# Gram products of 320-column rows: the last piece as columns 192 to 319 instead of 256 to 319

## The chip, the cores and the metric

The kernel runs on one core of a Trainium2 chip. The metric is the device time of one execution in microseconds; three runs of the kernel before gave 719.22, 720.55 and 721.73 us, with the median 720.55 us. A profile of one execution was taken as well.

## The reference

Three layers follow one another, in float32.

```python
# a recurrence over 768 steps, for 4 batches x 8 heads of 40
m_new = np.maximum(f_gate + m, i_gate)
f_stab, i_stab = np.exp(f_gate + m - m_new), np.exp(i_gate - m_new)
C = f_stab * C + i_stab * outer(v_t, k_t)
n = f_stab * n + i_stab * k_t
y_t = sigmoid(o_gate) * (C @ q_t) / max(abs(n . q_t), 1)
# x: the 3072 rows of 320 (8 heads x 40)
h = x @ w_in                                   # 320 -> 2048
x = (max(h, 0) + alpha * min(h, 0)) @ w_out    # 2048 -> 320
out = max(x @ w1, x @ w2, x @ w3) @ w4         # 320 -> 768 -> 320
```

The inputs are float32; the host passes the weights as 64-bit words, so each weight is a float64 that the kernel turns into float32 itself.

## The kernel before

**Parts.** The rows are cut into 24 tiles of 128 tokens and eight chunks of three tiles. For each tile the recurrence is computed in its chunked form ("attention": products q by k, a matrix of decays db, a carried state C). The result is transposed into xT. Then come, chunk by chunk, the units m1 (x by w_in, eight matmuls of 384 columns into one PSUM bank, 16 units a chunk), m2 (g by w_out), and four chunks later m3 (three products and a maximum, 18 units a chunk) and m4 (h by the last weight, w4). All large products are made of float16 parts with a high and a low half, for precision.

**Scales and Gram products.** To split a weight into float16 halves the kernel needs a power of two that bounds it. `Norms` (line 1172) finds one with TensorE: for each converted block of a weight it multiplies the block's transpose by the block itself, 128 columns at a time, and adds all of these in one PSUM bank; the diagonal then holds sums of squares of columns. `power` (line 1193) takes the largest entry, spreads it over the partitions by a product with ones, and halves the exponent. Only the exponent's bound matters. For w_in and the weights w1 to w3 the blocks have 512, 256 or 128 columns, so all pieces are 128 wide. In `prep_rows` (line 1258) the blocks are rows of 320 columns: 16 blocks of w_out and 6 of w4. Their pieces are columns 0 to 127, 256 to 319 (64 wide) and 128 to 255, in this order. In the profile and in the order these products are those whose only input is a buffer cv, qs or ks: the buffers in which a weight is converted.

**Order.** Nothing is issued as it is written. Each operation is recorded with its inputs and outputs (`Sched.add`, line 154), and `Sched.cost` (line 225) gives it a duration by its shape: a matmul's grows with its output columns. `Sched.order` (line 305) lays out the program with these durations, from six sets of starting values and in eight rounds each, and keeps the plan with the shortest planned end. The plan sets the order on all five queues (TensorE, DVE, ACT, POOL and the transfers of SP), which of the eight PSUM banks each product uses, on which of two engines some copies run, and where TensorE gets fillers: products of ones with themselves (line 569), put in front of an instruction where the plan has TensorE idle and its clock low. 26 fillers open the program; others follow only after the plan's first stretch.

So the cost of one product can move any instruction.

Of the kernel before, what the change touches and what calls it, by code (L numbers as in the profile page):

```python
# [585 lines left out]
def kernel(  # L586
# [26 lines left out]
    class Ring:  # L613
# [6 lines left out]
        def __call__(self):  # L620
            self.n += 1
            t = self.t + self.more
            return t[(self.n - 1) % len(t)]
# [548 lines left out]
    class Norms:  # L1172
# [6 lines left out]

        def __call__(self, v):  # L1180

            at = list(range(0, v.shape[1], 128))
            for c in sorted(at, key=lambda c: (c > 0, min(128, v.shape[1] - c))):
                w = min(128, v.shape[1] - c)
                pe.matmul(
                    out=self.ps[0:w, self.at, 0:w], lhsT=v[:, c:c + w], rhs=v[:, c:c + w],
                    start=(self.k == 0), stop=(self.k == self.n - 1),
                )
                self.k += 1
            if self.k == self.n:  # L1190
                self.at, self.k = self.at + 1, 0
# [167 lines left out]
    for j in range(NCH + LAG):  # L1359
# [20 lines left out]
        if j == AFTER[3]:  # L1380
            prep_rows(w4, wp_s, wp, 2, 4, 8, sbp)
            dve.scalar_tensor_tensor(
                out=kw, in0=rw[:, 7:8], scalar=ONE, in1=rw[:, 8:9], op0=ALU.mult, op1=ALU.mult
# [79 lines left out]
```

## Time and profile before

| what | value |
|---|---|
| median of the runs | 720.55 us (719.22 to 721.73) |
| span of the profiled execution | 717.8 us |
| from the span to the median | 2.75 us |
| TensorE (PE) | 685.9 us busy, 96% |
| weight loads (PEld) | 464.1 us, 65% |
| DVE | 484.9 us, 68% |
| ACT | 415.8 us, 58% |
| POOL | 159.4 us, 22% |
| mean granted clock of TensorE | 0.950 |

The profiled execution's own time is known by its span, from the first instruction to the last; what lies around it is taken as the distance to the median. The busy shares are means over stages: in the first hundred microseconds the weights are converted and the first tiles go through attention; then attention and the first layer's units run side by side; in the last half TensorE has nothing but large products. A granted clock of 1.0 is 2.4 GHz, 0.5 is 1.2 GHz. The durations of matmuls overlap, so what one costs is read from the distance between starts.

### The profile page before, as it was taken

What the parts mean: (1) busy time and instruction counts of PE and PEld (TensorE: products, weight loads), DVE (VectorE), ACT (ScalarE), POOL (GpSimd) and SP (SyncE); (2) the same over time, 40 slices, a digit from 0 to 9 for tenths busy, and PEclk for the clock granted to TensorE, in tenths of its full rate; (3) what the DMA queues carried; (4) which work ended last, traced back from release to release, by engine and by line L of the source; (5) the groups of instructions that cost most, each with busy time, mean ns of one, the idle gap of its engine ahead of it and who ended that gap; (6) DMA issues with size and microseconds to landing.
All of it is one profiled execution on the core that took longest, in us unless ns stands there. A gap on an engine that the chain in (4) does not pass through costs nothing.

```text
span 717.8 us, 14674 instructions
## 1 busy us (share of the span) xinstructions
PE 685.9 (96%) x5299; PEld 464.1 (65%) x5299; DVE 484.9 (68%) x1256; ACT 415.8 (58%) x983; POOL 159.4 (22%) x193
## 2 busy tenths in 40 slices
PE   4789999999899999999999999999999999999998
PEld 3678766666566666666666666666766676666665
DVE  7676879999799899899579963786265223242332
ACT  4667769899799889887467662662253122222222
POOL 1221242044251362166014310330031000000000
PEclk8555799999999999999999999999999999999999
DMA  8865476565794656863443362122201110002000
GB/s 251 280 189 188 154 225 190 165 194 161 230 292 123 203 168 182 244 190 92 104 137 119 122 136 88 45 64 38 59 19 33 28 50 12 28 1 61 8 21 27
DMA packets 82802, 88.33 MB, mean 123 GB/s; under 512 B 38754, under 2 KB 66218, under 8 KB 82730
## 3 DMA queue, kind: packets, MB, share of 16 engines
q1 hardware_dynamic: 82730, 87.40, 42.2%
q8 instruction: 41, 0.67, 0.4%
q14 instruction: 31, 0.25, 0.1%
HBM read 60.83 MB, written 8.75 MB: 97 GB/s over the span
## 4 chain that ended last, share of the span: by engine, by line
PE 59%; DVE 2%; issue 0%; DMA 0%; SPq 0%; ACT 0%; ACTq 0%
PE bank L574 59%; DMA cs<-cpd 0%; SPq L574 0%; DVE wq L574 0%; DVE h L574 0%; DVE hl L574 0%; DVE vw L574 0%; DVE g L574 0%; DVE cp L574 0%; ACT db L574 0%; DVE y L574 0%; DVE gf L574 0%; DVE xs L574 0%; DVE cv L574 0%; ACT ob L574 0%
## 5 line engine op out<-in xcount | busy, mean ns | idle before, releaser
L574 PE MATMUL bank<-xT,wi 128*128 128x384 f16 x1024 | 177.1, 328 | 0.2 <-DVE gf L574 0.2
L574 PE MATMUL bank<-wo,g 128*128 128x320 f16 x1152 | 165.3, 299 | 0.6 <-DVE g L574 0.6
L574 PEld LDWEIGHTS <-wq 128*128 128x128 f16 x1152 | 110.9, 98 | 71.2 <-issue 0.5
L574 PEld LDWEIGHTS <-g 128*128 128x128 f16 x1152 | 110.9, 98 | 44.8 <-DVE g L574 0.9
L574 PEld LDWEIGHTS <-wi 128*128 128x128 f16 x1024 | 98.8, 98 | 62.3 <-issue 2.0
L574 PE MATMUL bank<-x2T,wq 128*128 128x384 f16 x720 | 123.1, 326 | 0.4 <-DVE gf L574 0.4
L574 POOL TENSOR_TENSOR g<-gf,g 128x384 f16<-128x384 f32 x63 | 60.6, 964 | 174.1 <-DVE g L574 95.3
L574 DVE TENSOR_TENSOR mv<-bank,mv 128x384 f32<-128x384 f32 x96 | 52.9, 551 | 60.4 <-PE bank L574 59.5
L574 DVE SCALAR_TENSOR_TENSOR gf<-d,al,bank 128x384 f32<-128x384 f32 x128 | 76.5, 603 | 9.9 <-ACT d L574 9.1
L574 ACT ACTIVATE h<-mv 128x384 f16<-128x384 f32 x47 | 24.5, 521 | 94.1 <-DVE mv L574 94.1
L574 ACT ACTIVATE d<-bank 128x384 f32<-128x384 f32 x128 | 61.1, 479 | 20.1 <-PE bank L574 18.8
L574 PE MATMUL bank<-xT,wq 128*128 128x384 f16 x432 | 70.7, 326 | 0.0
L574 ACT ACTIVATE db<-db,gtok 128x128 f32<-128x128 f32 x192 | 63.4, 390 | 9.1 <-POOL db L574 8.9
L574 ACT ACTIVATE g<-gf 128x384 f16<-128x384 f32 x104 | 53.7, 519 | 20.0 <-DVE gf L574 19.7
L574 PE MATMUL bank<-wp,h 128*128 128x320 f16 x432 | 61.0, 299 | 0.0
L574 PEld LDWEIGHTS <-h 128*128 128x128 f16 x432 | 42.1, 98 | 16.7
L574 POOL TENSOR_TENSOR h<-mv,h 128x384 f16<-128x384 f32 x14 | 13.8, 983 | 161.1 <-ACT h L574 161.0
L574 DVE TENSOR_TENSOR g<-gf,g 128x384 f16<-128x384 f32 x65 | 39.2, 610 | 11.3 <-ACT g L574 11.1
L574 POOL TENSOR_SCALAR_AFFINE_SELECT db<-db 128x512 f32<-128x512 f32 x48 | 36.7, 784 | 40.5 <-ACT gm L574 25.8
L574 DVE TENSOR_TENSOR db<-bank,db 128x512 f32<-128x512 f32 x48 | 31.8, 682 | 7.3 <-PE bank L574 2.0
L574 DVE TENSOR_SCALAR sx<-sx 128x1 int32<-128x1 int32 x48 | 7.0, 146 | 40.5 <-ACT xs L574 40.2
L574 ACT ACTIVATE xs<-bank 128x320 f16<-128x320 f32 x24 | 10.3, 429 | 37.1 <-PE bank L574 36.5
(170 smaller groups left out, 890.3 us busy)
## 6 DMA issues: line engine op xcount, KB each, us to landing
db<-ddr SPq DMA_DIRECT2D x24, 512.0 KB
raw<-tok SPq DMA_DIRECT2D x18, 480.0 KB
kv<-tok SPq DMA_DIRECT2D x24, 320.0 KB
q<-qk SPq DMA_DIRECT2D x36, 160.0 KB
raw<-w_out SPq DMA_DIRECT2D x16, 320.0 KB
raw<-w SPq DMA_DIRECT2D x9, 512.0 KB
qs<-hl SPq DMA_DIRECT2D x54, 80.0 KB
ks<-hl SPq DMA_DIRECT2D x54, 80.0 KB
```

The source lines that it names most:

```text
L574: getattr(e, meth)(**{k: v.on(v.bank.tile) if isinstance(v, View) else v for k, v in kw.items()})
```

## The change

The pieces of a row are now taken in the order of their columns, and each is 128 wide: the last one of 320 columns starts at 192 instead of 256. Columns 192 to 255 are thus counted twice, and their sums of squares come out larger; the bound is still one. Blocks whose width is a multiple of 128 are cut as before.

```diff
         def __call__(self, v):
 
-            at = list(range(0, v.shape[1], 128))
-            for c in sorted(at, key=lambda c: (c > 0, min(128, v.shape[1] - c))):
-                w = min(128, v.shape[1] - c)
+            for c in range(0, v.shape[1], 128):
+                c = min(c, v.shape[1] - 128)
                 pe.matmul(
-                    out=self.ps[0:w, self.at, 0:w], lhsT=v[:, c:c + w], rhs=v[:, c:c + w],
+                    out=self.ps[:, self.at, :], lhsT=v[:, c:c + 128], rhs=v[:, c:c + 128],
                     start=(self.k == 0), stop=(self.k == self.n - 1),
                 )
                 self.k += 1
```

Since the recorded durations of 22 products differ, the plan differs from its first instructions on. Three places on TensorE's queue follow.

The first place is just ahead of the first m1 unit. Before, a row of w_out in cv is taken in three pieces, and then come 15 fillers, of which the first stands here, and the unit:

```order
L574 LDWEIGHTS cv_137
L574 MATMUL bank_66<-cv_137 128x128
L574 LDWEIGHTS cv_137
L574 MATMUL bank_66<-cv_137 64x64
L574 LDWEIGHTS cv_137
L574 MATMUL bank_66<-cv_137 128x128
L569 LDWEIGHTS ones
L569 MATMUL bank_67<-ones 128x256
```

Now attention products (C by q) and pieces of a row in ks stand there, and the unit follows at once:

```order
L574 MATMUL bank_69<-C_168,q_149 128x41 x4
L574 LDWEIGHTS ks_154
L574 MATMUL bank_66<-ks_154 128x128
L574 LDWEIGHTS ks_154
L574 MATMUL bank_66<-ks_154 128x128
L574 LDWEIGHTS wi_88
L574 MATMUL bank_65<-xT_130,wi_88 128x384
```

The fillers in front of the unit are gone from there; of 36 fillers behind the leading 26, 31 are left in the whole program.

The second place is earlier, where the scale of alpha goes through TensorE (ident with am, then ones with dg). Before, the product of dg stood ahead of attention's products of C, with nothing in between:

```order
L574 LDWEIGHTS ones
L574 MATMUL bank_63<-dm_187,ones 128x1
L574 LDWEIGHTS ones
L574 MATMUL bank_69<-dg_190,ones 128x4
L574 MATMUL bank_68<-C_168,q_149 128x41 x4
L574 MATMUL bank_64<-C_168,q_149 128x41 x4
L574 MATMUL bank_65<-va_161,db_158 128x41 x8
```

Now the C products, those of va and db, and eight of q for the next tile come first, of which the last two stand here; then ident with am, and ten fillers, of which the first stands here, ahead of dg:

```order
L574 MATMUL bank_69<-q_149 128x128
L574 MATMUL bank_66<-q_149 128x128
L574 MATMUL bank_68<-ident,am_180 1x128
L569 LDWEIGHTS ones
L569 MATMUL bank_65<-ones 128x256
```

The scale of alpha moved behind a whole tile's attention. With it moved the conversion of w_in (wi) on DVE and ACT.

The third place is late, where rows of w4 go between large units. Before, a 64-wide piece stands between a unit of m2 and one of m3:

```order
L574 LDWEIGHTS g_126
L574 MATMUL bank_66<-wo_108,g_126 128x320
L574 LDWEIGHTS cv_137
L574 MATMUL bank_68<-cv_137 64x64
L574 LDWEIGHTS wq_100
L574 MATMUL bank_65<-x2T,wq_100 128x384
```

Now all pieces there are 128 wide:

```order
L574 LDWEIGHTS wq_97
L574 MATMUL bank_63<-x2T,wq_97 128x384
L574 LDWEIGHTS cv_138
L574 MATMUL bank_66<-cv_138 128x128
L574 LDWEIGHTS wq_100
L574 MATMUL bank_67<-x2T,wq_100 128x384
```

The pieces still stand one by one between units; the units around them are others.

## Rows read from the trace of the kernel before

**Rows 1.** Stages: span; PE, PEld, DVE, ACT, POOL busy (instructions); PEclk, DMA share, GB/s.
```profile
0.00:47.50 47.50, 31.00 (x205) 25.69 (x206) 32.67 (x92) 24.98 (x61) 9.57 (x27) 0.62 0.81 249
47.50:101.70 54.20, 54.13 (x370) 41.82 (x370) 39.72 (x108) 37.47 (x86) 13.54 (x19) 0.67 0.63 190
101.70:326.00 224.30, 212.19 (x1872) 143.38 (x1872) 206.70 (x553) 199.97 (x493) 80.70 (x88) 1.00 0.67 192
326.00:714.60 388.60, 388.55 (x2856) 253.23 (x2854) 205.84 (x506) 152.82 (x346) 55.63 (x62) 1.00 0.22 59
sum 714.60, PE 685.87 PEld 464.12 DVE 484.92 ACT 415.25 POOL 159.44; mean PE 171.47 PEld 116.03 DVE 121.23 ACT 103.81 POOL 39.86
```
**Rows 2.** Chain of waits, its end: start, length (us), what.
```profile
324.48 390.08 PE bank L574 x2869
714.59 0.53 ACT ob L574
```
**Rows 3.** Timeline of TensorE in the fourth stage: start, length (us), instructions.
```profile
326.84 1.46 PE L574 MATMUL bank<-x2T,wq 128*128 128x384 f16 x8
328.14 0.22 PE L574 MATMUL bank<-cv 128*128 128x128 bf16 x1
328.19 1.46 PE L574 MATMUL bank<-x2T,wq 128*128 128x384 f16 x8
329.59 0.22 PE L574 MATMUL bank<-cv 128*64 128x64 bf16 x1
329.74 1.47 PE L574 MATMUL bank<-x2T,wq 128*128 128x384 f16 x8
```
**Rows 4.** Timeline of TensorE at half clock.
```profile
41.58 0.63 PE L574 MATMUL bank<-cv 128*128 128x128 bf16 x4
42.01 0.52 PE L574 MATMUL bank<-qs 128*128 128x128 bf16 x3
...
62.79 1.76 PE L574 MATMUL bank<-cv 128*128 128x128 bf16 x9
64.35 1.24 PE L574 MATMUL bank<-qs 128*128 128x128 bf16 x6
```
**Rows 5.** Groups of weight loads: count | busy us, mean ns | idle before.
```profile
L574 PEld LDWEIGHTS <-cv 128*128 128x128 bf16 x89 | 8.3, 106 | 4.9 <-DVE cv L574 2.1 <-issue 0.2
...
L574 PEld LDWEIGHTS <-cv 128*64 128x64 bf16 x12 | 1.4, 114 | 2.6 <-issue 2.5
```
**Rows 6.** Timeline of TensorE: the last fillers and the first m1 unit.
```profile
79.14 3.02 PE L569 MATMUL bank<-ones 128*128 128x256 bf16 x15
81.95 1.96 PE L574 MATMUL bank<-xT,wi 128*128 128x384 f16 x8
```
**Rows 7.** Timeline of TensorE: m1 units at both clock levels.
```profile
83.81 1.46 PE L574 MATMUL bank<-xT,wi 128*128 128x384 f16 x8
85.20 0.22 PE L574 MATMUL bank<-cv 128*64 128x64 bf16 x1
85.35 1.47 PE L574 MATMUL bank<-xT,wi 128*128 128x384 f16 x8
...
97.44 2.72 PE L574 MATMUL bank<-xT,wi 128*128 128x384 f16 x8
99.98 0.24 PE L574 MATMUL bank<-ks 128*128 128x128 bf16 x1
```
**Rows 8.** Timeline of DVE: waits for TensorE (idle before, by whom).
```profile
70.06 0.50 DVE L574 TENSOR_TENSOR num<-bank,num 128x328 f32<-128x328 f32 x1 [4.00 <-PE bank L574]
...
75.31 0.49 DVE L574 COPY xT<-bank 128x640 f16<-128x640 f16 x1 [2.27 <-PE bank L574]
```
**Rows 9.** Timeline: the product of dg on TensorE, and the long scan on DVE.
```profile
47.56 0.16 PE L574 MATMUL bank<-dg,ones 128*128 128x4 bf16 x1 [2.37 <-DVE dg L574]
...
8.46 1.27 DVE L574 TENSOR_TENSOR_SCAN h<-h 32x512 f32<-32x512 f32 x1
```

## The prediction

> **What bounds the kernel now.** I read first the table of stages, then the chain of waits, then the timeline of TensorE around the touched products. The table [rows 1] cuts the span into four. Up to 47.5 us TensorE is busy 31.00 us of 47.50 and waits for inputs. From 47.5 to 101.7 it is busy 54.13 of 54.20 us, at a mean granted clock of 0.67: a mix of 1.2 GHz (0.5) and 2.4 GHz (1.0), so about a third of this stage runs at the full level. From 101.7 to 326 it is busy 212.19 of 224.30 us, beside DVE with 206.70 and ACT with 199.97; 12.1 us are idle. From 326 to 714.6 it is busy 388.55 of 388.60 us at full clock. The chain of waits [rows 2] says the same: its last 390.08 us are one unbroken run of TensorE, and 0.53 us of ACT follow. So a microsecond taken off TensorE after 326 us is a microsecond of the span; one taken off between 47.5 and 101.7 us shortens that stage, and whether it reaches the end is decided in the third stage.
>
> **The change, part by part.** The products that change are the last pieces of rows of 320 columns: 16 of w_out (all before 101.7 us) and 6 of the last weight (all after 326 us), 22 in all. Pieces of the other weights are 128 wide before and after, and their order stays as well. Nothing is removed or added in number: 22 products write 128 columns instead of 64.
>
> *What a 64-wide product costs.* In the fourth stage [rows 3] such pieces stand alone between units of eight matmuls. From 326.84 to 328.19 us a unit and a 128-wide piece take 1.35 us; from 328.19 to 329.74 a unit and a 64-wide piece take 1.55 us. The narrow piece costs 0.20 us more, not less. Half of that stands ahead of it (its unit needs 1.40 us, from 328.19 to 329.59, against 1.30 us from 326.84 to 328.14), half behind (0.15 us to the next start against 0.05). At half clock [rows 4] nine pieces, three of them 64 wide, take 1.56 us from 62.79 to 64.35, while four full ones take 0.43 us from 41.58 to 42.01, or 0.97 for nine: (1.56 - 0.97) / 3 = 0.20 us again. Between units at 85.20 [rows 7] it is 1.54 us from 83.81 to 85.35, again about 0.2 above 1.35. So something is paid on entering and on leaving the narrow form.
>
> The rule in the Trainium skill that bears on this is that changing the tiling mode, not just the tile, drains TensorE (TensorEngine Tiling (Array Packing), Key Properties); the stretched starts on both sides of the narrow piece agree with it. A second rule speaks against the change: the time of a weight load goes with its columns, about columns / 1.2 ns (TensorE: Matmul & The Clock Gate, LDWEIGHTS (loading the stationary operand)). By it each of the 22 loads would grow by an estimated 53 ns, 1.2 us in all, and by it the sum would be a loss. The rows differ from it: the loads of 64 columns have a mean of 114 ns and those of 128 columns 106 ns [rows 5].
>
> *Sum of this part.* Six pieces after 326 us, each 0.20 us on a TensorE without idle time: 1.2 us. Sixteen before: at most 16 x 0.20 = 3.2 us. By the order three stand beside fp32 products that themselves use part of the array, where little or nothing can be saved, and two more are doubtful; 11 x 0.20 = 2.2 us is the lower end. I take 2.6 us, nearer to the lower end. What it frees is not TensorE's time alone: DVE waits for TensorE 4.00 us at 70.06 and 2.27 us at 75.31 [rows 8], and these waits shrink with it.
>
> *What the order does.* The costs that the planner sees have changed, so it lays the whole program out anew, and all five queues differ. The sums of work hardly do: DVE gets four instructions more, POOL four fewer, ACT as many, SP the same transfers in another order. At DVE's mean of 484.92 us over 1259 instructions [rows 1] four are 1.5 us, in a program that leaves DVE 17.6 us free in the third stage. Three moved pieces count:
> - Fillers (products of ones that keep TensorE busy): 36 beside the leading 26 before, 31 now. One costs 0.2 us at half clock (15 from 79.14 to 81.95 take 2.8 us [rows 6]). Five fewer: between 0 (they had filled idle time) and 1.0 us. I take 0.5.
> - The product of dg, for which TensorE waited 2.37 us at 47.56 [rows 9], now stands behind attention products and ten fillers. The wait should go; the ten fillers (2.0 us) stand in its place and are counted above. What is late next is the first m1 unit, which needs the third transposed tile. Gain between -2.0 and 2.4 us; I take 0, since filler and wait are about alike.
> - In the gates the scan of the first 256 steps now runs to its end before DVE starts the scan of 512 (1.27 us [rows 9]). That may bring the first attention tile forward by up to 1.3 us; the transfers to DRAM and back lie between, and I take 0. A loss of up to 1.3 us is possible in the same way for the second half.
>
> The moved transfers follow the moved steps in SP's queue. One of note: the two copies that swap the tail of xT now stand ahead of a load of decays (db) and four of q; these queue behind the third xT tile. While that tile is not late they cost nothing; each microsecond of lateness would be passed on to the attention tile behind.
>
> *The third stage*, rearranged in small steps throughout, cannot be priced from rows of before: its 12.1 us of idle could shrink by a few or grow by as many. I take no change and +-4 us.
>
> Sum: 1.2 + 2.6 + 0.5 = 4.3 us off the profiled span of 717.8 us gives 713.5 us. The median of the runs, 720.55 us, lies 2.75 us above that span; the same stretch on top gives 716.3 us.
>
> **Rivals.**
> *The early gain is swallowed.* In the third stage DVE is busy 92% and ACT 89% [rows 1]; if these two set its end, TensorE arrives earlier and idles longer. Only the six late pieces are left: 720.55 - 1.2 = 719.4 us. For it: the two shares. Against: DVE's own idle time before 101.7 us is partly waiting for TensorE [rows 8], so it arrives earlier as well.
>
> *Slower: the first m1 units run at half clock.* Before, 15 fillers stand right in front of the first unit [rows 6], the units from 83.81 us on take 1.39 us for eight matmuls, and the one that fell into a stretch at 0.5 takes 2.54 us (97.44 to 99.98) [rows 7]. In the new order no filler precedes the first unit; 18 stand far ahead of it, 13 between later units. If eight of the first units run at the low level, this costs 8 x 1.15 = 9.2 us, and the time is 720.55 - 4.3 + 9.2 = 725.5 us. It decides from six units on (6.9 us, 723.2 us). For it: the low level held for most of the stage [rows 1]. Against: in the trace the full level was back by the second unit [rows 6, 7], and the units themselves are the densest work there is.
>
> *Wider pieces cost more.* If a narrow piece had cost half of a full one (0.107 us at half clock [rows 4]), 22 would add 22 x 0.054 = 1.2 us: 721.7 us. The weight-load rule named above would bring this about. All of rows 3 to 5 speak against it.
>
> *Faster still: the new order starts earlier.* If the dg wait goes (2.4 us) and its fillers fall into idle time, and the scan's 1.3 us arrives, 4.3 + 2.4 + 1.3 = 8.0 us: 712.6 us.
>
> **How the numbers follow.** A change under 0.3%, 2.2 us, cannot be told from none: faster is below 718.4, slower above 722.7 us. Chances: the forecast 0.50, with its own range 713 to 719 us (0.46 faster, 0.04 within); swallowed 0.20 (0.03 faster, 0.17 within); slower by the clock 0.16; wider costs 0.03 (within); the early order 0.11 (faster). Together 0.60 faster, 0.24 within, 0.16 slower. The range goes from 710 us, the early order with a third stage a little better, to 723 us, where the slower rival begins; about 0.1 lies beyond each end at most.
>
> **What would show it.** In the profile after: no form 128*64 among the pieces; units with a piece between them at 1.35 us after 326 us; three-piece runs at half clock in 0.32 instead of 0.52 us; 57 fillers in all; the run that ends the chain shorter by about 1.2 us for the same work; TensorE's stage without idle ending some 3 us earlier. Wrong would be: pieces that keep the 0.2 us, a first row of m1 units above 2 us each, or TensorE's idle time between 100 and 330 us above 15 us.

## The result: 0.9% slower, with pieces that are cheaper as forecast

The changed kernel takes 725.83 us (median of 6, 724.71 to 729.11), the kernel before 719.88 us in the same session (median of 6, 718.13 to 722.05). The ratio is 1.0091, 95% interval 1.0063 to 1.0119. The forecast was 716.3 us with a range of 710 to 723; the time lies above the range. The profiled run of the changed kernel has a span of 722.8 us, 5.0 more than before.

The table of stages of the changed kernel, columns as in [rows 1]:

```profile
0.00:47.50 47.50, 33.19 (x219) 28.02 (x220) 34.80 (x89) 24.34 (x59) 10.27 (x27) 0.61 0.80 247
47.50:101.70 54.20, 51.67 (x363) 41.75 (x364) 42.05 (x119) 37.83 (x87) 14.43 (x17) 0.69 0.64 196
101.70:326.00 224.30, 211.53 (x1816) 140.82 (x1815) 207.15 (x538) 195.36 (x476) 70.65 (x78) 0.97 0.67 187
326.00:719.50 393.50, 393.05 (x2903) 256.99 (x2900) 209.47 (x517) 158.56 (x362) 60.19 (x68) 1.00 0.23 61
```

Read the third line against [rows 1]: TensorE is busy about as long as before (211.53 against 212.19 us), but gets through 56 instructions fewer (1816 against 1872), and its mean granted clock is 0.97 instead of 1.00. Busy time alone hides this loss.

The end of the chain of waits (start, length, what), against [rows 2]:

```profile
293.94 425.13 PE bank L574 x3134
719.09 0.53 ACT ob L574
```

TensorE's last wait now ends at 293.94 us, 30 us earlier than before, and yet the last product comes 4.5 us later (719.09 against 714.59). So the loss is older than 293.94 us.

The pieces themselves, on the timeline of TensorE (start, length, instructions), against [rows 3]:

```profile
344.87 1.46 PE L574 MATMUL bank<-x2T,wq 128*128 128x384 f16 x8
346.17 0.22 PE L574 MATMUL bank<-cv 128*128 128x128 bf16 x1
346.23 1.46 PE L574 MATMUL bank<-x2T,wq 128*128 128x384 f16 x8
347.53 0.22 PE L574 MATMUL bank<-cv 128*128 128x128 bf16 x1
347.59 1.46 PE L574 MATMUL bank<-x2T,wq 128*128 128x384 f16 x8
```

A unit and a piece take 1.36 us in both cases shown; the step of 1.55 us is gone. The beginning of the first linear layer, against [rows 6, 7]:

```profile
75.51 5.74 PE L574 MATMUL bank<-xT,wi 128*128 128x384 f16 x24
81.09 0.33 PE L574 MATMUL bank<-ks 128*128 128x128 bf16 x3
...
85.62 4.45 PE L574 MATMUL bank<-xT,wi 128*128 128x384 f16 x16
89.91 0.22 PE L574 MATMUL bank<-cv 128*128 128x128 bf16 x1
...
98.27 0.16 PE L574 MATMUL bank<-dm,ones 128*128 128x4 bf16 x1 [1.12 <-DVE dm L574]
98.29 0.38 PE L569 MATMUL bank<-ones 128*128 128x256 bf16 x2
98.51 2.65 PE L574 MATMUL bank<-va,db 128*128 128x41 f32 x16
100.96 2.76 PE L574 MATMUL bank<-xT,wi 128*128 128x384 f16 x8
103.52 0.84 PE L569 MATMUL bank<-ones 128*128 128x256 bf16 x3
```

The first unit starts at 75.51 us instead of 81.95: an early lead of 6.4 us. Then come units that run wholly or mostly at 1.2 GHz: two (16 matmuls) in 4.29 us from 85.62 to 89.91, one in 2.56 us from 100.96 to 103.52. Two waits of the third stage have half clock behind them too:

```profile
185.15 0.61 PE L574 MATMUL bank<-qs,ks 120*128 120x128 f16 x4 [3.81 <-DMA ks<-hl]
...
293.94 0.16 PE L574 MATMUL bank<-dm,ones 128*128 128x1 bf16 x1 [2.57 <-DVE dm L574]
293.96 2.72 PE L574 MATMUL bank<-x2T,wq 128*128 128x384 f16 x8
296.48 2.23 PE L574 MATMUL bank<-wo,g 128*128 128x320 f16 x12
```

And the stretches themselves in the table of windows (columns as above):

```profile
85.70:89.20 3.50, 3.50 (x13) 1.69 (x12) 3.13 (x9) 2.11 (x8) 0.63 (x1) 0.51 0.76 217
99.40:106.20 6.80, 6.80 (x27) 4.18 (x27) 6.37 (x20) 4.84 (x11) 2.38 (x2) 0.50 1.07 259
184.70:188.10 3.40, 2.95 (x22) 2.51 (x23) 2.30 (x4) 1.43 (x3) 0.87 (x1) 0.50 1.11 211
294.00:297.40 3.40, 3.40 (x13) 1.70 (x13) 3.37 (x18) 3.10 (x8) 0.00 (x0) 0.50 0.32 107
```

The two traces can be laid side by side by the work that TensorE has done. The changed kernel is 5.2 us ahead where before stands at 83 us, 0.7 behind at 106, 0.3 ahead at 143, 6.3 behind at 186, 7.7 behind at 293 to 313, 5.6 at 325, and 4.5 from 376 us on. So the early lead is lost before the third stage is well under way, and the third stage loses again.

A second sum tells in what form the time went. Of each instruction's time to the next start, idle time is taken off; half of what lies under a granted 0.5 counts as lost to the clock; the rest is fillers or products at full clock. In us, from the traces (e1 and p1 are experiments below):

```
                      idle   clock  fillers  products   sum
before                28.7   29.1     9.4     647.1    714.3
changed               29.6   35.3     8.8     645.1    718.8
e1 (wide, old plan)   28.9   29.2     8.9     643.7    710.7
e2 (narrow, new plan) 30.1   32.3     8.8     648.3    719.5
p1 (changed, mended)  28.3   30.3    10.5     646.1    715.1
```

The products became cheaper by 2.0 us and the fillers by 0.6; the clock took 6.2 us, idle time 0.9. This is the form in which the time went; whether the low clock is also the cause is a question for the experiments.

These are single traces. The granted clock of every run is known too, and span times (1 - clock) is what a run lost to it, idle time under 0.5 included. Its mean is 35.7 us of a span of 719.3 for the kernel before (134 runs in the sessions of the experiments, standard deviation 2.6 us; one run in a slower state is left out) and 41.8 of 724.7 us for the changed kernel (6 runs). What is left is 683.6 and 682.9 us: in the mean of the runs, too, the loss has the form of the clock.

### The profile page after: what moved, and what is told of

The parts are those of the page before. It is cut to its first block, busy times and chain, and to the rows that moved or that the text cites. A ratio compares the mean times of both kernels' runs of the same rounds, so it can differ in the third digit from the quotient of the medians.

```text
span 722.8 us, 14648 instructions
## 1 busy us (share of the span) xinstructions
PE 689.4 (95%) x5294; PEld 467.6 (65%) x5294; DVE 493.5 (68%) x1260; ACT 416.2 (58%) x983; POOL 155.5 (22%) x189
## 4 chain that ended last, share of the span: by engine, by line
PE 71%; ACT 8%; DVE 8%; DMA 5%; issue 5%; SPq 3%; POOL 0%; DVEq 0%; ACTq 0%; POOLq 0%
PE bank L574 71%; SPq L574 3%; ACT db L574 2%; DMA q<-qk 1%; DVE wo L574 1%; ACT xs L574 1%; ACT g L574 1%; DMA ks<-hl 1%; DMA cs<-cpd 1%; DVE db L574 1%; ACT d L574 1%; DVE gf L574 1%; DMA h<-ig 1%; DVE xs L574 1%; ACT hl L574 1%
## 5 line engine op out<-in xcount | busy, mean ns | idle before, releaser
L574 PE MATMUL bank<-xT,wi 128*128 128x384 f16 x1024 | 180.5, 333 | 0.5 <-DVE xs L574 0.4
L574 PEld LDWEIGHTS <-wi 128*128 128x128 f16 x1024 | 100.4, 100 | 67.1 <-issue 6.7
L574 POOL TENSOR_TENSOR g<-gf,g 128x384 f16<-128x384 f32 x65 | 62.8, 967 | 212.9 <-ACT g L574 114.5
L574 ACT ACTIVATE h<-mv 128x384 f16<-128x384 f32 x44 | 22.9, 521 | 89.5 <-DVE mv L574 89.4
L574 POOL TENSOR_TENSOR h<-mv,h 128x384 f16<-128x384 f32 x13 | 12.0, 927 | 182.6 <-ACT h L574 177.7
L574 POOL TENSOR_SCALAR_AFFINE_SELECT db<-db 128x512 f32<-128x512 f32 x48 | 34.8, 745 | 37.7 <-ACT gm L574 28.1
L574 DVE TENSOR_TENSOR g<-gf,g 128x384 f16<-128x384 f32 x63 | 36.0, 582 | 9.2 <-ACT g L574 9.0
```

The lines of the kernel that those rows point to most:

```text
L574: getattr(e, meth)(**{k: v.on(v.bank.tile) if isinstance(v, View) else v for k, v in kw.items()})
```

## The experiments

Ratios are to the kernel before in the same session (its medians: 721.08, 721.38, 722.50, 720.92 and 721.33 us), with 95% intervals.

**Width and plan taken apart.** The planner lays the program out by its cost of each product, so the source cannot change a piece without changing the plan. A recorded product was therefore given a second set of operands, used only when it is issued:

```
+ if w < 128:                       # in Norms: recorded 64 wide, as before
+     r = v[:, c + w - 128:c + w]
+     real = dict(out=self.ps[:, self.at, :], lhsT=r, rhs=r)
...
+ kw = {**kw, **kw.get("real", {})} # in issue(); e2 the other way round
```

e1, wide pieces in the plan of before:

> The 22 last pieces are issued 128 wide (columns 192 to 319), but the planner still sees them 64 wide and in the old place, so all five queues stand word for word as before. Theory A (the plan costs, the width saves): six pieces in the last stage save 0.20 us each, 1.2 us, and sixteen early ones 2 to 3 us, of which most arrives: 715.5 to 717.5 us against 719.9 before. Theory B (the width itself costs, by weight loads or columns): 721 to 726 us. Theory C (early savings are swallowed by the third stage): 718.5 to 719 us, with the last stage alone 1.2 us shorter.

Measured 715.16 us, 0.9910 [0.9878, 0.9942]. e2, narrow pieces in the changed kernel's plan:

> The plan of the changed kernel, word for word on all queues, but of each row of 320 columns the middle product is issued 64 wide (columns 256 to 319) and the last one as columns 128 to 255: the width is undone, the plan is kept. Theory A: the plan costs about 10 us and the width saves 3 to 4, so 728 to 731 us against 725.8 for the changed kernel. Theory B: 718 to 721 us. Theory C: 727 us.

Measured 727.84 us, 1.0078 [1.0044, 1.0113]. The slowdown belongs to the plan: all five queues of e1 stand as before and it gains; e2 has the 64-wide pieces back and still loses. Between e2 and the changed kernel the products differ by 3.2 us for 22 pieces, 0.15 us each, in the direction forecast; the clock took 3.0 us of it back in that pair of traces, and by the ratios (1.0078 and 1.0091) the two cannot be told apart. Without what each run lost to the clock the means are 680.3 us for e1 (8 runs) against 683.6 before, and 682.9 for the changed kernel against 686.4 for e2 (8 runs): the width is worth 3.3 and 3.5 us, each give or take 1 us, in either plan. In e2 a narrow piece still needs its 1.54 us (346.17 to 347.71), where the changed kernel needs 1.36:

```profile
346.17 1.46 PE L576 MATMUL bank<-x2T,wq 128*128 128x384 f16 x8
347.56 0.22 PE L576 MATMUL bank<-cv 128*64 128x64 bf16 x1
347.71 1.47 PE L576 MATMUL bank<-x2T,wq 128*128 128x384 f16 x8
```

**The two terms in the old plan.** `sc.narrow` counts the pieces as recorded; only those above 16 (l1), or up to 16 (l2), are issued wide.

```
+ sc.narrow = getattr(sc, "narrow", 0) + (w < 128)
- if w < 128:
+ if w < 128 and sc.narrow > 16:    # l2: <= 16
```

> The plan of before word for word, with only the six late pieces (those after 326 us) 128 wide. By the forecast's first term 6 x 0.20 = 1.2 us: ratio to before 0.998, every row ahead of 326 us as before. If the early sixteen carry nothing through the third stage (rival: swallowed), the whole gain of 0.9% that all 22 gave would have to be here: ratio 0.991.

> The plan of before word for word, with only the sixteen early pieces (those ahead of 101.7 us) 128 wide. By the forecast's second term 2.6 us (2.2 to 3.2): ratio to before 0.996 (0.9955 to 0.997), with the late pieces still at 0.20 us each. All 22 together gave 0.991, so 0.9925 if the rest is all early. Rival (the early gain is swallowed in the third stage): ratio 1.000.

l1: 719.66 us, 0.9995 [0.9965, 1.0024]. l2: 716.76 us, 0.9953 [0.9928, 0.9978], 3.4 us. The sixteen early pieces carry their gain through the third stage when the plan stays; the gain of the six late ones is too small to be told from nothing by the times, and their 1.2 us stands in the traces alone.

**Other plans.** One or two nanoseconds in the planner give another plan:

```
+ if meth == "matmul" and kw["lhsT"].shape[1] == 64 and kw["lhsT"].dtype == BF16:
+     dur += 1.0                    # j1; j2: 2.0, both from the kernel before
...
- ("pe", "act"): 267.0
+ ("pe", "act"): 268.0              # k1; k2: 266.0, both from the changed kernel
```

> The kernel before with the same 64-wide pieces; only the planner's cost of the 22 pieces is 1 ns more, which gives another plan (51 fillers for 62) of the same work. Theory A (the loss is what any new plan may bring or take: its waits and its stretches at half clock): a time off 719.9 us by several us in either direction, 715 to 730. Theory D (the new plan is bad because wide pieces are planned in; plans of the same pieces are alike): 718 to 722 us.

> As the one with 1 ns, with 2 ns more in the planner's cost of the 22 pieces: a third plan (72 fillers). Theory A: another time again, anywhere in 715 to 730 us, not tied to the number of fillers. Theory D: 718 to 722 us.

> The changed kernel (22 pieces 128 wide) with another draw of the plan: the planner's latency from TensorE to ACT is 268 instead of 267 ns, and all five queues come out otherwise (48 fillers instead of 57). Theory A (what the plan happens to be is worth more than the pieces): anywhere between 715 and 728 us; the three narrow plans other than that of before stood at 724 to 728, and 3 us less for the width gives 721 to 725. If the wide pieces themselves made plans worse, 725.8 or above. If the plan of after were an unlucky one of its kind, 718 or below.

> The changed kernel with a third draw of its plan: the planner's latency from TensorE to ACT is 266 instead of 267 ns (72 fillers instead of 57). The five plans other than that of before that have run (after, the narrow pieces in it, two with narrow pieces, one with wide) stood at 1.003 to 1.009 of the kernel before. If the plan of before is simply the best of those drawn, 1.002 to 1.009 again; if wide pieces gave good plans as often as bad ones, below 0.998 is as likely as not.

j1 (narrow): 727.13 us, 1.0070 [1.0043, 1.0097]. j2 (narrow): 724.36 us, 1.0045 [1.0014, 1.0075]. k1 (wide): 724.40 us, 1.0030 [1.0008, 1.0052]. k2 (wide): 722.72 us, 1.0021 [0.9997, 1.0045]. Five plans other than that of before have now run, counting the changed kernel's: by its ratio none beats it, whichever pieces they hold (k2's interval still includes no change), and they spread over 0.7%. That is nearly as much as the whole change cost. j1 and j2 are the kernel before with a changed guess about 22 products; by their ratios they lose 3 to 5 us without any change in what is computed.

**What in the new plan costs.** f1 puts fillers into the two long waits, f2 into the early ones as well, f3 takes the waits away by moving what stands ahead:

```
+ sc.fill[1344] = (32, 1)           # f1: fillers, bank; ahead of the product of ks
+ sc.fill[1560] = (21, 0)           #     ahead of the product of dm
+ sc.fill[646] = (2, 6)             # f2: these as well
+ sc.fill[651] = (8, 6)
...
+ for i in (2256, 1904):            # f3: two units ahead of the product of dm
+     move(i, 1560)
+ for i in (2239, 2240, 2241):      #     x2T's transposes, later on SP
+     move(i, 1162)
+ for i in (2242, 2243):            #     x2T's swap copies
+     move(i, 1692)
```

> The changed kernel with its own plan, and 53 fillers more: 32 ahead of the attention product for which TensorE waited 3.81 us at 185.15, 21 ahead of the power product for which it waited 2.57 us at 293.94. At 107 ns each they fit into the waits (3.4 and 2.2 us), so nothing is late by them and the waits' ends stay. Theory C (a wait in the third stage costs twice, once itself and once through the half clock that follows it): the stretches at half clock from 184.7 to 188.1 and from 293.96 to 297.4 are gone, 1.7 us each, 3.4 us in all: 722.4 us, ratio to the changed kernel's 725.8 about 0.995, ratio to the kernel before 1.004. Rival R (the third stage is set by DVE, ACT and the transfers; TensorE's clock there is swallowed by the next wait): within 1 us of 725.8, ratio to before 1.008, whatever the granted clock. Rival F (the fillers are in the way): slower than 726.5 us.

> As the run with fillers in the two late waits, and ten more fillers at 96.8 and 98.27 us, ahead of the products that waited 0.33 and 1.12 us there (1.1 us of fillers). Theory C: the half clock from 99.4 to 106.2 us goes as well, up to 3.4 us more, of which the next waits may take some: 719 to 721 us, ratio to before about 0.999. Rival R: no change against the changed kernel, 725.8 us. If the ten fillers do not bring the full level back there, the time is that of the run without them, 722.4 us.

> The changed kernel with the two waits themselves moved away, no filler added: the three transposes of x2T and the two copies that swap its tail (4.9 us of SP's queue between 158.7 and 176) are issued some 45 us later, where SP is idle and still 45 us before their use, so that the loads of ks behind them are issued earlier; and two units (x2T,wq and wo,g) stand ahead of the power product of dm instead of behind it. Theory C: the wait of 3.81 us shrinks to 0 to 1.5 us, that of 2.57 goes, and the half clock behind both goes (3.4 us): 6 to 9 us less than 725.8, so 717 to 720 us, ratio to before 0.994 to 0.999. Rival R: other waits take their place, and the time stays within 1.5 us of 725.8. If only the clock matters and not the waits, the same 722.4 us as with fillers.

f1: 725.65 us, 1.0071 [1.0042, 1.0099]; f2: 726.18 us, 1.0071 [1.0041, 1.0101]; f3: 726.00 us, 1.0066 [1.0039, 1.0093]. All three missed: 3 to 9 us were expected, 0.2 to 0.25% (1.4 to 1.8 us) came, which the intervals do not tell from nothing. Yet each did what it says at its place. In f1 the products of ones fill the wait, and the unit behind runs at the full level, 1.30 us (296.25 to 297.55) instead of 2.52:

```profile
293.49 2.46 PE L569 MATMUL bank<-ones 128*128 128x256 bf16 x21
296.23 0.16 PE L574 MATMUL bank<-dm,ones 128*128 128x1 bf16 x1 [0.28 <-DVE dm L574]
296.25 1.46 PE L574 MATMUL bank<-x2T,wq 128*128 128x384 f16 x8
297.55 1.79 PE L574 MATMUL bank<-wo,g 128*128 128x320 f16 x12
```

In f2 the unit after the early wait takes 1.31 us (102.53 to 103.84) instead of 2.56:

```profile
102.53 1.47 PE L574 MATMUL bank<-xT,wi 128*128 128x384 f16 x8
103.84 0.49 PE L569 MATMUL bank<-ones 128*128 128x256 bf16 x3
```

So a full clock behind a wait is not yet time won: the fillers stand where the idle time stood, and what is waited for does not come earlier. In f2 TensorE still waits 0.21 us for ks and 0.28 us for dm behind the fillers, so they are not in the way; its clock is full from 83.9 us on; and yet it loses no less in the third stage than the changed kernel (5.9 against 4.9 us from 106 to 325, in the table behind p1). In the mean of their runs f1 and f2 lost 38.4 and 37.5 us to the clock, 3.4 and 4.3 less than the changed kernel, and took as long.

In f3 a new cost shows on SP's queue (start, length, instructions): the three transposes, side by side now, take 6.36 us instead of 3.87, ahead of loads of weight rows.

```profile
207.12 6.36 SPq L574 DMA_TRANSPOSE x2T<-x2d  x3
213.59 2.06 SPq L574 DMA_DIRECT2D raw<-w  x3
```

I then took VectorE for the engine that sets the pace, since it is busy for 207 of 224 us in the third stage and, by its trace, 8 us longer than before up to the 25th of the steps that write xs from y, sx and xs (226.4 against 218.4 us, at 265.3 and 260.4 us). Work was added in e1's plan and taken from the changed kernel's; g2 and g3 leave out 320 of the 384 columns of each chosen step:

```
- for meth, kw in op.calls:
+ for meth, kw in op.calls * (2 if i in self.chosen else 1):     # g1: 8 gf, g4: 5 units, n2: both
...
+ if i in self.chosen:                                           # g2, g3: 16 gf
+     kw = {k: v[:, 0:64] if hasattr(v, "ap") and v.shape[-1] == 384 else v for k, v in kw.items()}
```

> The wide pieces in the plan of before (715.16 us in its run), with eight of the steps gf<-d,al,bank on VectorE issued twice, spread over the third stage (about 150 to 250 us): 8 x 0.53 us = 4.2 us more on VectorE, the same result. Theory D (from about 100 to 300 us VectorE sets the pace: what is added to it moves the whole chain of attention, and TensorE's end with it): the 25th of the last steps xs<-y,sx,xs moves from 260 to about 263.5, and the time rises by 3 to 4.2 us, to 718 to 719.4, ratio to before about 0.996. Rival T (TensorE with its waits and its clock sets it, VectorE has 8% idle that takes the steps up): at most 1 us more, 715 to 716, ratio 0.991 to 0.993.

> The wide pieces in the plan of before, with five of the units xT,wi (eight matmuls each, 1.30 us) issued twice in the third stage: 6.5 us more on TensorE, the same result. Theory D: TensorE has some 10 us of idle time between 100 and 326 us there, and part of the 6.5 us is taken up by it: 1 to 4 us more than 715.2, so 716 to 719, ratio 0.993 to 0.998. Rival T (TensorE sets the pace throughout): the full 6.5 us, 721.7, ratio 1.000 to 1.001.

> All 22 pieces wide in the plan of before, with 4.2 us more on VectorE (eight steps gf twice) and 6.5 us more on TensorE (five units twice) in the third stage, together in one kernel. Apart they gave ratios of 0.9921 and 0.9912, against 0.991 without: next to nothing. Theory of shared slack (some microseconds of slack exist once, for all engines together): more than the sum of the two, 718 to 722 us, ratio 0.996 to 1.001. If each engine has its own slack: as apart, 715 to 717, ratio 0.991 to 0.993.

> The changed kernel in its own plan, with 16 of the steps gf<-d,al,bank on VectorE in the third stage done on 64 of their 384 columns (the other columns keep old values): 16 x 0.33 to 0.40 = 5 to 6 us less on VectorE. Theory D: the 25th step xs<-y,sx,xs comes 4 to 5 us earlier than 265.3, and the time falls by 3 to 5 us from the changed kernel's 725.8: 721 to 723, ratio to before 1.000 to 1.003. Rival T: no change, 725 to 726, ratio 1.007 to 1.009.

> As the run with 16 shorter steps on VectorE, and the two TensorE waits moved away as well (which by itself gave nothing: 726.0 us). Theory D: once VectorE is relieved the two waits are worth something again, 1 to 4 us more: 718 to 721, ratio to before 0.996 to 1.000. Rival T: 725 to 726, as without. If the relief alone gives everything, the same 721 to 723 as without the moves.

g1: 714.84 us, 0.9921 [0.9889, 0.9953]. g4: 716.30 us, 0.9912 [0.9878, 0.9947]. n2: 718.64 us, 0.9946 [0.9919, 0.9974]. Against e1's 0.9910 neither 4.2 us on VectorE nor 6.5 us on TensorE can be told from nothing, and both together, 10.7 us, cost some 0.4%, within what the intervals leave open. The full price of TensorE's work (0.9%) is far outside the intervals, that of VectorE's (0.58%) just outside. The traces say the same of VectorE: with the added work the 25th step comes at 261.2 us (g1) and 258.6 (n2), against 260.0 in e1 and the 263.5 that theory D gave. So neither engine alone sets the pace of the good plan, and theory D falls as I put it. TensorE's idle time seems to give way: in the third stage n2 is busy 217.19 us and e1 214.18; but the traces of n1 and l2, which have the same plan without added work, stand at 209.81 and 214.40.

```profile
101.70:326.00 224.30, 217.19 (x1917) 145.82 (x1916) 208.45 (x544) 194.86 (x477) 79.18 (x86) 1.00 0.67 189
```

g2: 725.88 us, 1.0026 [0.9998, 1.0055], though its median is 1.0047 of that of before; g3: 724.30 us, 1.0050 [1.0023, 1.0076]. Relief on VectorE may be worth up to 0.6% in the new plan; the two runs disagree on how much. In g2's trace VectorE has 5.6 us less work up to the 25th step (220.8 against 226.4 us), and the step comes at 266.4 us, not 4 to 5 us earlier than 265.3 as expected; so these traces do not show VectorE's work as what holds the chain up. n1 puts the changed kernel's order on SP into e1:

```
+ move(2239, 1097); move(2240, 1097); move(2241, 1376)   # x2T's transposes
+ move(2242, 1029); move(2243, 1357)                     # x2T's swap copies
```

> All 22 pieces wide in the plan of before, with five steps on SP's queue moved to where the changed kernel has them: the three transposes of x2T and the two copies that swap its tail stand between the loads of qs and of ks of the same tile, some 1.1 to 3.6 us of SP's time ahead of the ks loads; all else as in the run with the wide pieces in the old plan (715.16 us). Theory S (SP's order is a cause): the wait for ks at 180 us grows from 1.33 to 3 to 5 us, and the time rises by 2 to 5 us, 717 to 720, ratio to before 0.994 to 0.998. Rival (the stage's slack takes it up): 715 to 716, ratio 0.991 to 0.992.

n1: 716.80 us, 0.9942 [0.9917, 0.9967]. The wait for ks grew to 2.90 us, nearly the 3 to 5 expected, and in this trace no half clock followed in the whole third stage:

```profile
190.75 0.61 PE L576 MATMUL bank<-qs,ks 120*128 120x128 f16 x8 [2.90 <-DMA ks<-hl]
...
101.70:326.00 224.30, 209.81 (x1872) 141.13 (x1871) 204.08 (x536) 194.90 (x479) 79.32 (x86) 1.00 0.66 189
```

The time rose by 0.3%, against intervals of that width: SP's order costs at most part of the loss.

**Three causes at once.** p1 moves the transposes behind the loads of weight rows, so that the cost seen in f3 goes, keeps f3's other moves, and has f2's ten early fillers:

```
+ sc.fill[646] = (2, 6)
+ sc.fill[651] = (8, 6)
...
+ for i in (2256, 1904):
+     move(i, 1560)
+ for i in (2239, 2240, 2241):
+     move(i, 1433)
+ for i in (2242, 2243):
+     move(i, 1692)
```

> The changed kernel with three of its losses taken away together: the x2T transposes and swap copies issued later (here behind the loads of the next weight rows, so that they hold nothing up), two units ahead of the power product of dm, and the ten fillers at 96.8 and 98.27 us that in an earlier run brought the full clock back between 99.4 and 106.2. If the loss is a sum of small ones: 3 to 6 us less than the changed kernel's 725.8, ratio to before 1.000 to 1.004. If each one is replaced by another wait, as when they were taken away singly: 1.005 to 1.009.

p1: 722.08 us, 1.0022 [0.9999, 1.0045], where the changed kernel stands at 1.0091 [1.0063, 1.0119]; the intervals do not touch. Its clock stays at 2.4 GHz from 83.4 us on:

```profile
83.40:101.70 18.30, 17.45 (x163) 13.60 (x160) 17.79 (x44) 17.22 (x40) 7.18 (x7) 1.00 0.75 212
101.70:326.00 224.30, 211.85 (x1866) 141.94 (x1865) 211.51 (x549) 198.72 (x487) 74.38 (x81) 1.00 0.67 190
326.00:717.00 391.00, 389.31 (x2855) 254.28 (x2855) 206.49 (x509) 156.15 (x355) 58.02 (x65) 1.00 0.22 61
```

In the third stage it does 1866 instructions where the changed kernel did 1816, in the same busy time. In the table of sums (3.7 us less in all for this pair of traces) the clock falls by 5.0 us and idle time by 1.3, for 1.7 us more of fillers and 1.0 of products. So three moves together give back three quarters of the loss by the ratios (0.69 of 0.91%).

Where each of them acts can be read from the traces. The work of TensorE is divided at the places where the kernel before stands at 47.5, 83, 106, 180, 200, 293 and 325 us; the table has the time that each trace takes for the same work, less that of the kernel before, in us:

```
          0-47.5  47.5-83  83-106  106-180  180-200  200-293  293-325  325-end
changed    -2.5    -2.8      6.0     0.0      3.1      3.9     -2.1     -1.0
f1         -1.5    -0.2      5.6    -0.7      2.4      2.7     -1.8     -1.0
f2         -0.7    -1.8      2.4     1.3      2.8      3.8     -2.0     -1.0
f3         -2.5    -2.4      3.6     0.6      0.0      5.4      1.5     -1.0
p1         -2.6    -0.2      2.2     0.9      0.2      0.5      0.9     -1.0
e2         -1.5    -0.7      3.5     0.5      1.9      3.0     -1.5     -0.1
```

The wait for ks lies in the part from 180 to 200: it costs 3.1 us, with fillers in it still 2.4 and 2.8, and nothing once the loads come earlier (f3, p1). The wait for dm and the transposes' new place lie in the part from 200 to 293: fillers take off 1.2 us (f1) or nothing (f2), f3 loses more than the changed kernel, and p1 is 4.9 us better than f3. The early fillers stand in the part from 83 to 106 (f2, p1). So it is the waits that cost in the third stage, and the half clock behind them is the form of a part of the cost. Up to 83 us the traces of the changed kernel's plan differ by up to 3.6 us, and part of what is won at one place is lost at the next, from 293 to 325 us above all; so these sums tell the places, from one trace each, and not shares of the ratio. e1 remains the version that beats both kernels.

## Why the prediction was wrong

The step that failed is the one on the new order, at two places. The forecast has 3.1 us won ahead of the third stage (2.6 + 0.5), no change in it, and 1.2 us won behind it. By the work done, the changed kernel is 0.7 us behind at 106 us, 5.6 behind at 325 and 4.5 behind at the end: 3.8 us are missed ahead of the third stage, 4.9 in it and 0.1 behind it, 8.8 in all (4.3 ahead forecast, 4.5 behind in the traces).

The larger part is the step on the third stage: "cannot be priced from rows of before: its 12.1 us of idle could shrink by a few or grow by as many. I take no change and +-4 us". It lost 4.9 us, and 7.0 up to 293 us. The measure was wrong as well as the size. Idle time, which I bounded, hardly moved in sum: 12.8 us are idle in that stage now, against 12.1. What is new is where TensorE waits, 3.81 us for ks and 2.57 us for dm, and the half clock behind it, 5.4 us in that stage where the kernel before lost none. f2 has no half clock there and loses no less (5.9 us from 106 to 325 us), so it is the waits that the sum had to price.

The smaller part is ahead of it: the early gain of 3.1 us, for which "What the order does" took 0 for each moved piece. The gain came (5.2 us ahead at 83 us) and was gone at 106: the part from 83 to 106 us took 6.0 us longer, with some 10 us at half clock (85.7 to 89.2 and 99.4 to 106.2) where the kernel before has 3.4.

*What a 64-wide product costs: right.* 0.20 us at the late places by the traces (1.55 or 1.54 against 1.36 us); 0.15 us on average over 22 in the pair of e2 and the changed kernel. Nine pieces at half clock, three of them former narrow ones, take 0.96 us, 0.32 for three, as the forecast said, instead of 1.56 [rows 4]:

```profile
67.93 1.16 PE L574 MATMUL bank<-cv 128*128 128x128 bf16 x9
68.89 0.84 PE L574 MATMUL bank<-qs 128*128 128x128 bf16 x6
```

The forecast had 3.8 us for all (1.2 and 2.6), 0.53%. In the unchanged plan e1 gained 0.9%, and 0.53% lies just outside its interval; 2.6 us of e1's gain are the clock of its runs (33.1 us lost against 35.7), 3.3 us the rest.

*Six late pieces, 1.2 us: right by the trace.* The lag falls from 5.6 us at 325 to 4.5 at the end in the changed kernel; e2, with narrow pieces in the same plan, keeps its lag there.

*Sixteen early pieces, 2.6 us: right.* 3.4 us in l2 (interval 1.6 to 5.2), and they reach the end there. This refutes the first rival, an early gain that is swallowed, for the plan of before.

*Fillers, 0.5 us: right.* 57 are left, and the sums put their share at 0.6 us less.

*The wait for dg: right about its place, and its successor early.* The product now stands at 58.70 us and waits 0.69 us instead of 2.37 [rows 9]. VectorE's waits for TensorE between 60 and 80 us fell from 7.4 to 5.6 us in sum, and the first unit came 6.4 us earlier [rows 6]; what share of that each has was not measured. That is the start which the fourth rival, an earlier order, described; but nothing of it was left at 106 us.

*The slower rival: right about the mechanism, half right about the place.* It gave 725.5 us for eight first units at half clock; 725.83 us were measured. The units at 85.62 and 100.96 us are such units; but two fifths of the time at half clock after 83 us (6.8 of 17.1 us) lie behind the two long waits of the third stage, at 185 and 294 us, which the rival did not name. Its price of 1.15 us for a unit at half clock was a little low, since the 1.39 us it took for the full level has a narrow piece behind it: 2.56 against 1.30 us is 1.26. That the time comes out so close is partly luck: the clock took 6.2 us, not 9.2.

*Wider pieces cost more: refuted.* Loads of 128 columns from cv have a mean of 108 ns now, and e1 is faster by 0.9%. The rule of the Trainium skill that bears on it (TensorE: Matmul & The Clock Gate, LDWEIGHTS (loading the stationary operand)) puts 128 columns at an estimated 107 ns, which these rows agree with, and 64 columns at 53 ns, which they do not: the loads of 64 columns took 114 ns [rows 5].

```profile
L574 PEld LDWEIGHTS <-cv 128*128 128x128 bf16 x101 | 9.5, 108 | 6.5 <-DVE cv L574 3.5 <-issue 0.4
```

*What would show it wrong* was too narrow: "TensorE's idle time between 100 and 330 us above 15 us" did not come true (12.8), and of the m1 units the first three stay under 2 us each (1.86, 75.51 to 81.09), the next two do not (2.15). The granted clock of the third stage and the work done by its end belonged on that list.

I treated a new plan as the old plan with a few moved pieces. Five plans within 0.7% of each other, all behind the one of before by their ratios, show that the plan was the largest term, and an unknown one; its bound of 4 us stood beside the sum, but not in the chance for slower.

What stays open: how the 5 us between the changed kernel and p1 divide in the times (the traces tell the places alone), what the 1.1% between p1 and e1 consists of (the 8 us of VectorE's work were a candidate, but g2 took 5.6 of them away and the 25th step came no earlier), and why none of the five plans matches the old one; that it is a lucky draw among many would explain it, and six plans are too few to show that.

## What to carry to other kernels

Where a cost feeds a planner, a change of a product is two changes; measure the product with the plan held fixed, and the plan with the product held fixed, before judging either. In a stage where three engines are busy for over 85% of the time, do not look at busy and idle time alone: compare the instructions done and the granted clock per stage, and the time that the same work takes. A low clock behind a wait does not make the clock the cause: fill the wait, and see whether time comes back. And when removing single waits gives nothing, remove several together before calling the cause refuted.

## What the hardware showed that I had not expected

The fall of the clock does not follow from the length of a wait alone: after 2.57 and 3.81 us of idle time (changed kernel) the level was 0.5, after 2.90 us (n1) it stayed at 1.0. Nor does the plan settle it: ahead of the same product of the same plan TensorE was idle for 2.31 us in the kernel before, up to 196.08 us, and the level stayed at 1.0; in l2 it was idle for 2.23 us, up to 192.24, and the level was 0.5 from 192.4 to 195.8 us. Three transposes issued back to back on SP held the queue 6.36 us (f3) and 5.64 us (p1), where two and one apart took 2.67 and 1.20 us in the changed kernel; what makes them longer was not tested:

```profile
158.69 2.67 SPq L574 DMA_TRANSPOSE x2T<-x2d  x2
...
162.02 1.20 SPq L574 DMA_TRANSPOSE x2T<-x2d  x1
```
